# Attention and multiplicative feed-forward on one core: the k·v product of the next batch moved into the two-level gates, in front of a q·kv product

## The chip, the cores and the metric

One core of a Trainium2 chip runs the whole program in one launch. The metric is the device time of that core in microseconds (us), median of the runs shown. All matrix products are float32. The engines are named as in the profile: PE (TensorE; PEld its weight loads), DVE (VectorE), ACT (ScalarE), POOL (GpSimd), SP (SyncE, which here issues most DMAs).

## The reference, cut to what matters

```python
batch, n_heads, seq, head_dim = (8, 8, 576, 64)
kv  = np.einsum('bhsd,bhse->bhde', k, v)          # 64x64 per head and batch
out = np.einsum('bhsd,bhde->bhse', q, kv)
rms = np.sqrt(np.mean(out * out, axis=-1, keepdims=True) + 1e-06)
x   = (out / rms * g_norm)                        # -> (8*576 tokens, 512)
a = x @ w1                                        # 512 -> 1024
b = x @ w2
h = a * b @ w3                                    # 1024 -> 1024
return h @ w_out                                  # 1024 -> 512
```

No step is non-linear between `w3` and `w_out`, so the kernel multiplies these two once, at the start, and then has two products per token: the gates (x times w1 and w2, multiplied elementwise) and the projection (times w3·w_out).

## The kernel before, in words

**Groups.** The 4608 tokens are worked on in nine groups of 512. Groups T = 0 to 6 and T = 7 hold the first 512 tokens of one batch each; T = 8 holds the 64 tokens left over of all eight batches. The order (`groups`, L1135) is 0, 1, ..., 6, 8, 7. While group T goes through its gates, the attention of batch b = T + 1 is computed in pieces in between, by `steps(b)` (L573).

**Fewer products by Strassen-Winograd.** The gates and the projection are written as seven products of half-size blocks instead of eight (`winograd`, L698). For T in `IN_TWO` (2 to 6, 8 and 7) the gates of the first three quarters of the features use two such levels, 49 products for 64 (`gates_of_two`, L948, matmuls of 128x128 by 128 columns at L976), with a one-level `gates` call for feature part p = 2 ahead of them and one for p = 3 behind them (128x128 by 256 columns, L708). Then `project_twice` (L1189) does the projection in two levels (L1223).

**Pieces.** Each of the three gate stages calls `between()`, which runs the next piece of `steps(b)`: pieces 0 and 1 in the gates of p = 2; pieces 2 to 5 in the two-level gates (after the third and the sixth of seven products, for each of w1 and w2); pieces 6 and 7 in the gates of p = 3. For b > 2 (`in_two`) they hold: piece 1, `begin_kv(1)` and `finish(0)` of batch b; piece 3, for odd b, `product_left` (L423, matmul L432); piece 4, `finish(1)`; piece 6, `begin_kv(0)` of batch b + 1.

**What these do.** `begin_kv(g)` (L480) calls `kv(g)` (L326): 36 matmuls of 64x64 (L335) into two PSUM banks, then six small ACT copies into `kv_sb` (L343, L345), and issues the loads of the next k and v (L104, on SP). `finish(h)` calls `product(h)` (L399): 32 matmuls of 64x64 (L413) into two banks, and `norm` (L374): per bank an ACT square (L380) and a DVE reduction (L381), then an ACT square root (L385), a DVE reciprocal (L387) and two DVE multiplications (L390). For b > 2 both squares go to one buffer, `sq0`, so that the second waits for the first reduction.

**PSUM.** Eight banks in two pools: `ps_mm` with five and `ps_at` with three. The two-level gates hold all five of `ps_mm`; of these `mm[0]` is used last by the second product of the second half (`plan`, L951), and read by `add_seven` (L1029, L1030). `product(1)` takes both its banks from `ps_at` for b > 2, and the `winograd` call of p = 3 takes its first bank, r1, from `ps_mm`.

**What sets the order.** PE, POOL and SP run in the order of the code. DVE runs in the order of the code from the gates of p = 3 to the end of the projection, and in an order that a planner makes elsewhere; ACT always in an order that the planner makes. In `gates` a DVE addition (L859) and multiplication (L860) make each block of the result; ACT copies (L726) keep the intermediate sums. Behind them, on DVE, come the sums that the projection reads: for its first product `sum_inner(0)`, for its second and third `sum_inner(1, 2)` (L1181, L1182, L1183 and L1185; the second call is the one of 128x512), and the sums over the first three feature parts (L1069 to L1072).

Of the kernel before, what the change touches and what calls it, by code (L numbers as in the profile page):

```python
# [22 lines left out]
def kernel(  # L23
# [36 lines left out]
    B, H, S, D = q.shape  # L60
# [4 lines left out]
    FIRST_OF_TWO = 2  # L65
# [18 lines left out]
    def bank(pool, tag):  # L84
        return pool.tile([P, 512], FP32, name=tag, tag=tag)
# [28 lines left out]
    NF = KF // 2  # L114
# [203 lines left out]
    def attention(b):  # L318
# [80 lines left out]
        def product(h):  # L399

            of_mm = b and not (h and b > FIRST_OF_TWO)
            o_ps = [bank(*((ps_mm, "mm") if of_mm else (ps_at, "at"))), bank(ps_at, "at")]
            for m in range(4):
                r, e = 2 * h + m // 2, m % 2
                for i in range(2):
                    n = 2 * m + i
                    for t in range(2):
                        tokens = slice(t * L, (t + 1) * L)  # L410
                        for l in range(2):
                            rows = slice(l * D, (l + 1) * D)
                            nc.tensor.matmul(  # L413
                                o_ps[l][tokens, n * D:(n + 1) * D],
                                lhsT=qT[r][rows, e, i, tokens],
                                rhs=kv_b[rows, m // 2 ^ l, e, h, :],
                                start=True,
                                stop=True,
                            )
            xn = st[h] = work.tile([P, 2, 2, 4, D], FP32, name="xn", bufs=1)  # L420
            return norm(o_ps, [xn[:, :, l].rearrange("p i m d -> p m i d") for l in range(2)])
# [90 lines left out]
    def batch(b):  # L512
        if b not in batches:
            batches[b] = attention(b)
        return batches[b]
# [57 lines left out]
    def steps(b):  # L573

        a = batch(b)
        a.start()
        more = b + 1 < B  # L580
        fs, ends = ([[] for _ in range(8)] for _ in range(2))

        def turn(i, f, *args, next_group=False):

            t = []

            def begin():
                t.append(f(*args))
                next(t[0])
                next(t[0])  # L590

            fs[i].append((begin,))
            (to_end if next_group else ends[i + 1]).append((lambda: all_of(t[0]),))

        if to_end:

            ends[0] += [(lambda: nc.gpsimd.tensor_copy(tick, late["p5"][:, 0, 0:1]),), *to_end]
        to_end.clear()
        odd = b % 2
        by_scalar, in_two = b >= FIRST_OF_TWO, b > FIRST_OF_TWO  # L600
        if b == 1:
            early.extend(a.q_two_by_dma(r) for r in (0, 1))
            q_first = list(early)
            fs[0].append((a.begin_kv, 0))

            def end_first():
                for t in q_first:
                    with tc.issue_after(copies["u3"][-1].ins):
                        next(t)
                    all_of(t)  # L610

            ends[1].append((end_first,))
        fs[2 if b == 1 else 1] += [(a.begin_kv, 1), (a.finish, 0)]
        if b == 1:
            last = {}

            def begin(name, behind, f, *args):
                last[name] = f(*args)
                with tc.issue_after(copies[behind][-1].ins):
                    next(last[name])  # L620
                next(last[name])

            def end(name, behind):
                with tc.issue_after(copies[behind][-1].ins):
                    next(last[name], None)
                all_of(last[name])

            fs[2] += [(begin, f"q{r}", "u2", a.q_two_by_dma, r) for r in (2, 3)]
            fs[3].append((begin, "left", "u3", a.q_left_by_dma))
            fs[4].append((begin, "x", "u3", a.x_by_dma, 0, nc.scalar.copy))  # L630
            ends[4] += [(end, "q2", "p1"), (end, "q3", "p5")]
            ends[5] += [(end, "x", "u2"), (end, "left", "u3")]
        elif by_scalar:
            turns_by_scalar(b)
        else:
            turn(1, a.q_two_by_dma, 2, 3)
            turn(2, a.x_by_dma, 0)
            if odd:
                turn(1, a.q_left_by_dma)
        second = 5 if b == 1 else 4  # L640
        if more:
            fs[6 if in_two else second].append((batch(b + 1).begin_kv, 0))
        fs[second].append((a.finish, 1))
        if odd:
            fs[3 if in_two else second + 1].append((a.product_left,))
        if b == 1:
            turn(6, a.x_by_dma, 1)
            turn(7, a.x_left_by_dma, next_group=True)
        else:
            if not by_scalar:  # L650
                turn(5, a.x_by_dma, 1)
            if odd:
                turn(5, a.x_left_by_dma, next_group=more)
        if more and not by_scalar:
            turn(7 if b == 1 else 5, batch(b + 1).q_two_by_dma, 0, 1, next_group=True)
        if more:
            fs[7 if odd else 0].append((load_q_left, b + 1))
        return iter([lambda s=e + f: [f(*args) for f, *args in s] for e, f in zip(ends, fs)])
# [38 lines left out]

    def winograd(  # L698
        lhsT, rhs, chunks, done, between=lambda: None, keep_u3=True, after=lambda: None,
        places=(2, 1),  # L700
    ):


        def product(a_name, b_name, to=None):
            ps = to if to is not None else bank(ps_mm, "mm").rearrange("p (u n) -> p u n", u=2)
            for u in range(2):
                for c in range(chunks):
                    nc.tensor.matmul(  # L708
                        ps[:, u, :],
                        lhsT=lhsT(a_name, u, c),  # L710
                        rhs=rhs(b_name, c),

                        start=(u == 0 and c == 0 and to is None),
                        stop=(c == chunks - 1),
                        skip_group_check=True,
                    )
            after()
            return ps

        def keep(name, ps):  # L720
            if name == "p1":
                t = pair_of_sums[:, 0].rearrange("p s c t -> p (s c) t")
            else:
                t = late_slots(places[name != "p5"])
            t = t[:, 0:4, :].rearrange("p (u a) n -> p u (a n)", u=2)
            copies.setdefault(name, []).append(nc.scalar.copy(t, ps))  # L726
            run_slot((stage[0], name), copies[name][-1])
            late[name] = t
            return t

        r1 = product("a11", "b11")
        p1 = keep("p1", r1)
        r2 = product("s1", "t1")
        p5 = keep("p5", r2)
        product("s2", "t2", r1)
        u2 = keep("u2", r1)
        between()
        product("s4", "b22", r2)
        done("c12", r2, u2)
        product("s3", "t3", r1)  # L740
        done("c22", p5, keep("u3", r1) if keep_u3 else r1)
        r3 = product("a12", "b21")
        done("c11", r3, p1)
        between()
        product("a22", "t4", r1)
        done("c21", r1, None)
# [97 lines left out]
    def gates(T, p, between, ready=lambda name: None):  # L844
        def done(name, one, two):
            multiply(name, one, two)
            ready(name)

        def multiply(name, one, two):

            dst = ab[int(name[1]) - 1][:, p, int(name[2]) - 1, :]
            if two is None:
                c = late_pool.tile([P, N], FP32, name="c21")
                copied = nc.scalar.copy(c, one[:, 0, :])  # L854
                run_slot((stage[0], name), copied)
                adds.setdefault(name, []).append(nc.vector.tensor_mul(dst, c, one[:, 1, :]))
                return
            c = late_pool.tile([P, 2, N], FP32, name="c")
            adds.setdefault(name, []).append(nc.vector.tensor_add(c, one, two))  # L859
            nc.vector.tensor_mul(dst, c[:, 0, :], c[:, 1, :])  # L860

        winograd(
            lambda name, w, c: wa[p][name][:, w, c, :],
            lambda name, c: xb[T][name][:, c, :],
            NP // 2, done, between, T == 0 or p + 1 < NF,
            places=(2, 1) if T not in IN_TWO else (0, 1) if p + 1 == NF else (2, 0),
        )


# [721 lines left out]
```

## Time and profile before

| | |
|---|---|
| median of 3 runs (lowest, highest) | 747.46 us (747.32, 747.8) |
| the profiled execution: its own time | 747.49 us |
| its span, first to last instruction | 745.7 us |
| granted TensorE clock | 1.000 |
| POOL busy | 21.8 us, 3% of the span |
| largest group by line: L708 matmuls from `xT`, `w_sb` | x480, 110.2 us |

The profiled execution's time is 1.8 us longer than its span; that part lies outside of the first and last instruction. Each float32 matmul of the code shows as two matmul records in the trace. A record's duration contains the pipeline behind it, so that records overlap: how long work takes on PE is read from start to start. In a row of the timeline, "x16" means that 16 records of one kind follow each other, the first number is the start in us from the span's start, the second how long the row lasts.

| group | T = 2 | T = 3 | T = 4 | T = 5 | T = 6 |
|---|---|---|---|---|---|
| batch of the pieces, b | 3 | 4 | 5 | 6 | 7 |
| `product(1)` in the two-level gates, start | 270.60 | 343.57 | 417.37 | 490.35 | 564.15 |
| k·v of b + 1 in the gates of p = 3, start | 283.32 | 356.30 | 430.10 | 503.07 | none |

### The profile page before, as it was taken

What the parts mean: (1) busy time and instruction counts of PE and PEld (TensorE: products, weight loads), DVE (VectorE), ACT (ScalarE), POOL (GpSimd) and SP (SyncE); (2) the same over time, 40 slices, a digit from 0 to 9 for tenths busy, and PEclk for the clock granted to TensorE, in tenths of its full rate; (3) what the DMA queues carried; (4) which work ended last, traced back from release to release, by engine and by line L of the source; (5) the groups of instructions that cost most, each with busy time, mean ns of one, the idle gap of its engine ahead of it and who ended that gap; (6) DMA issues with size and microseconds to landing.
All of it is one profiled execution on the core that took longest, in us unless ns stands there. A gap on an engine that the chain in (4) does not pass through costs nothing.

```text
span 745.7 us, 16754 instructions
## 1 busy us (share of the span) xinstructions
PE 737.6 (99%) x6843; PEld 658.4 (88%) x6843; DVE 633.1 (85%) x1212; ACT 371.3 (50%) x638; POOL 21.8 (3%) x29
## 2 busy tenths in 40 slices
PE   8999999999999999999999999999999999999998
PEld 6455788888899999999999999999999999999997
DVE  7987998957868699979996999799969987997797
ACT  6787868424552575256526752575267313212321
POOL 0000000132000000010000000000001000000000
PEclk9999999999999999999999999999999999999999
DMA  9996944499999689867986898579847662465454
GB/s 319 364 313 207 258 104 124 124 325 298 283 307 327 167 219 269 310 167 234 279 280 168 253 295 270 175 244 279 277 106 218 207 225 87 157 229 165 134 199 135
DMA packets 135456, 169.65 MB, mean 228 GB/s; under 512 B 78036, under 2 KB 110804, under 8 KB 135380
## 3 DMA queue, kind: packets, MB, share of 16 engines
q1 hardware_dynamic: 132928, 154.16, 68.9%
q10 hardware_dynamic: 2452, 14.42, 5.7%
q8 instruction: 54, 0.88, 0.5%
q14 instruction: 22, 0.18, 0.1%
HBM read 130.55 MB, written 20.71 MB: 203 GB/s over the span
## 4 chain that ended last, share of the span: by engine, by line
PE 92%; DVE 3%; DMA 3%; ACT 1%; issue 0%; SPq 0%; POOL 0%; ACTq 0%; DVEq 0%
PE mm L708 36%; PE mm L1223 22%; PE mm L976 21%; PE mm L682 7%; PE at L335 2%; PE at L413 1%; DMA raw<-in_moe_w_out_dram 1%; DMA w3o_sb<-w3o_l 1%; PE at L669 1%; PE mm L413 1%; DVE c L859 1%; DMA raw<-in_moe_w_dram 0%; DVE w_sb L172 0%; DMA out_dram<-raw 0%; PE at L1266 0%
## 5 line engine op out<-in xcount | busy, mean ns | idle before, releaser
L1025 ACT COPY slots<-mm 128x512 f32<-128x512 f32 x88 | 51.6, 586 | 131.8 <-PE mm L1223 73.7
L708 PE MATMUL mm<-xT,w_sb 128*128 128x256 f32 x480 | 110.2, 379 | 0.0
L708 PEld LDWEIGHTS mm<-xT,w_sb 128*128 128x128 f32 x480 | 90.4, 190 | 12.1 <-issue 0.5
L708 PE MATMUL mm<-xc,ws 128*128 128x256 f32 x352 | 79.8, 380 | 0.0
L708 PEld LDWEIGHTS mm<-xc,ws 128*128 128x128 f32 x352 | 66.9, 190 | 9.4 <-ACT inner_sums L726 0.4
L726 ACT COPY slots<-mm 128x512 f32<-128x512 f32 x61 | 35.7, 586 | 76.7 <-PE mm L708 54.6
L682 PE MATMUL mm<-chunks,ab 128*128 128x512 f32 x128 | 60.8, 606 | 0.6 <-DVE chunks L172 0.6
L1029 DVE TENSOR_TENSOR slots<-mm,slots 128x512 f32<-128x512 f32 x66 | 45.3, 686 | 17.7 <-PE mm L976 17.3
L1026 ACT COPY slots<-mm 128x384 f32<-128x384 f32 x88 | 42.4, 482 | 24.9 <-PE mm L1223 22.3
L976 PE MATMUL mm<-ws,w3o_sb 128*128 128x128 f32 x350 | 54.0, 275 | 0.0
L1223 PE MATMUL mm<-w3o_sb,ab 128*128 128x128 f32 x368 | 48.7, 275 | 0.5 <-DMA w3o_sb<-w3o_l 0.5
L381 DVE TENSOR_REDUCE inv<-sq 128x8 f32<-128x512 f32 (+1 forms) x40 | 24.6, 629 | 26.4 <-ACT sq L380 26.2
L976 PEld LDWEIGHTS mm<-ws,w3o_sb 128*128 128x128 f32 x350 | 46.4, 192 | 0.0
L1223 PEld LDWEIGHTS mm<-w3o_sb,ab 128*128 128x128 f32 x368 | 45.4, 192 | 1.1 <-issue 0.7
L1223 PE MATMUL mm<-w3o_sb,raw 128*128 128x128 f32 x340 | 43.5, 275 | 0.0
L708 PE MATMUL mm<-xc,w_sb 128*128 128x256 f32 x176 | 42.5, 385 | 0.9 <-ACT slots L726 0.9
L682 PEld LDWEIGHTS mm<-chunks,ab 128*128 128x128 f32 x128 | 21.6, 190 | 22.3 <-issue 14.3
L1223 PEld LDWEIGHTS mm<-w3o_sb,raw 128*128 128x128 f32 x340 | 40.7, 192 | 0.0
L708 PE MATMUL mm<-xT,ws 128*128 128x256 f32 x160 | 38.5, 384 | 0.0
L708 PEld LDWEIGHTS mm<-xc,w_sb 128*128 128x128 f32 x176 | 32.7, 190 | 6.3 <-ACT slots L726 1.7
L1030 DVE TENSOR_TENSOR slots<-mm,slots 128x384 f32<-128x384 f32 x66 | 36.4, 552 | 0.9 <-PE mm L1223 0.9
L854 ACT COPY c<-mm 128x256 f32<-128x256 f32 x22 | 8.2, 371 | 53.7 <-PE mm L708 53.7
(230 smaller groups left out, 1634.8 us busy)
## 6 DMA issues: line engine op xcount, KB each, us to landing
w3o_sb<-w_l SPq DMA_DIRECT2D x21, 896.0 KB, 5.5
w3o_sb<-w3o_l SPq DMA_DIRECT2D x18, 896.0 KB, 4.6
raw<-in_moe_w_dram SPq DMA_DIRECT2D x31, 512.0 KB, 7.5
raw<-w3o_l SPq DMA_DIRECT2D x15, 896.0 KB, 4.9
w3o_sb<-w3o_l ACTq DMA_DIRECT2D x14, 896.0 KB, 5.1
k_sb<-in_k_dram SPq DMA_DIRECT2D x16, 576.0 KB, 4.6
v_sb<-in_v_dram SPq DMA_DIRECT2D x16, 576.0 KB, 6.2
q_sb<-in_q_dram SPq DMA_DIRECT2D x32, 256.0 KB, 4.4
```

Source lines behind the costliest of these rows:

```text
L335: nc.tensor.matmul(ps[r * D:(r + 1) * D, :], lhsT=k_sb[rows, r, cols], rhs=v_sb[rows, r, cols], start=(j == 0), stop=(j == JS - 1),)
L381: adds["norm"] = nc.vector.tensor_reduce(out=inv[:, i], in_=sq.rearrange("p (h d) -> p h d", d=D), axis=AX.X, op=ALU.add)
L413: nc.tensor.matmul(o_ps[l][tokens, n * D:(n + 1) * D], lhsT=qT[r][rows, e, i, tokens], rhs=kv_b[rows, m // 2 ^ l, e, h, :], start=True, st ...
L682: nc.tensor.matmul(sums_ps[half][m], lhsT=w3T[half, c][:, m, :], rhs=chunks[:, c, 1, :], start=(c == 0), stop=(c == KF - 1),)
L708: nc.tensor.matmul(ps[:, u, :], lhsT=lhsT(a_name, u, c), rhs=rhs(b_name, c),  start=(u == 0 and c == 0 and to is None), stop=(c == chunks ...
L726: copies.setdefault(name, []).append(nc.scalar.copy(t, ps))
L976: nc.tensor.matmul(ps[place // 4][:, place % 4, :], lhsT=x, rhs=y, start=new and place // 4 not in seen, stop=True, skip_group_check=True,)
L1025: nc.scalar.copy(z[:, 0:4], ps[0])
L1026: return nc.scalar.copy(z[:, 4:7], ps[1][:, 0:3])
L1029: nc.vector.tensor_add(z[:, 0:4], ps[0], z[:, 0:4])
L1030: nc.vector.tensor_add(z[:, 4:7], ps[1][:, 0:3], z[:, 4:7])
L1223: nc.tensor.matmul(ps[place // 4][:, place % 4, :], lhsT=x[:, c, :], rhs=y[:, c, :], start=new and place // 4 not in seen, stop=(c == 1), ...
```

## The change

For b = 3 to 6, that is in groups T = 2 to 5, `begin_kv(0)` of batch b + 1 moves from piece 6 to piece 4, directly in front of `finish(1)`. So the k·v matmuls, which stood alone in the gates of p = 3, now stand directly ahead of the q·kv matmuls in the two-level gates. This needs two banks of `ps_at` at that place, and so the banks are dealt differently: `product(1)` of these batches takes its first bank from `ps_mm` (it gets `mm[0]`), and the first bank of the `winograd` call of p = 3 comes from `ps_at`. By the same condition batch 0, at the start of the program, takes the first bank of its two products from `ps_mm`.

```diff
-            of_mm = b and not (h and b > FIRST_OF_TWO)
+            of_mm = b < B - 1 or h == 0
             o_ps = [bank(*((ps_mm, "mm") if of_mm else (ps_at, "at"))), bank(ps_at, "at")]
...
         if more:
-            fs[6 if in_two else second].append((batch(b + 1).begin_kv, 0))
+            fs[second].append((batch(b + 1).begin_kv, 0))
         fs[second].append((a.finish, 1))
...
-        places=(2, 1),
+        places=(2, 1), first=None,
...
         def product(a_name, b_name, to=None):
-            ps = to if to is not None else bank(ps_mm, "mm").rearrange("p (u n) -> p u n", u=2)
+            new = to is None or to is first
+            ps = bank(ps_mm, "mm").rearrange("p (u n) -> p u n", u=2) if to is None else to
...
-                        start=(u == 0 and c == 0 and to is None),
+                        start=(u == 0 and c == 0 and new),
...
-        r1 = product("a11", "b11")
+        r1 = product("a11", "b11", to=first)
         p1 = keep("p1", r1)
+        first = None
...
             places=(2, 1) if T not in IN_TWO else (0, 1) if p + 1 == NF else (2, 0),
+            first=(
+                bank(ps_at, "at").rearrange("p (u n) -> p u n", u=2)
+                if T in IN_TWO and p + 1 == NF and T + 2 < B else None
+            ),
```

In the built programs, per changed group: on PE the 36 matmuls of L335 stand ahead of the 32 of L413, and the gates of p = 3 are without them. On ACT the six copies of L343 and L345 stand ahead of the first square (L380) of `finish(1)`. On SP the two loads of L104 stand ahead of the transposition of the left-over tokens (odd b) and of the first three loads for the projection (L1152), instead of behind the four transpositions of the gates of p = 3. The order on DVE and on POOL is the same.

## The prediction, made before the changed kernel was run

> **What bounds the kernel now.** I read the page first: its busy line, then the chain that ended last, then the timelines of PE, DVE and ACT around every 64x64 product.
>
> ```profile
> PE 737.6 (99%) x6843; PEld 658.4 (88%) x6843; DVE 633.1 (85%) x1212; ACT 371.3 (50%) x638; POOL 21.8 (3%) x29
> PE 92%; DVE 3%; DMA 3%; ACT 1%; issue 0%; SPq 0%; POOL 0%; ACTq 0%; DVEq 0%
> ```
>
> PE sets the end: it is busy 99% of the span and 92% of the chain lies on it. A us that PE no longer spends is gained, as long as no other engine makes it wait in its place. DVE, at 85%, is the one to watch. In the timeline of PE from group T = 2 on, starts follow each other at fixed steps: 16 records of 128x256 take 3.46 us (241.35 to 244.81), 0.216 each; 12 of 128x128 take 1.34, 0.112 each. The steps are broken in two kinds of place only: around 64x64 products, and once in group T = 6.
>
> **What the change takes from PE.** The first view is the timeline of PE around the k·v product alone, in the last gates of T = 2:
>
> ```profile
> 279.77 3.62 PE L708 MATMUL mm<-xc,ws 128*128 128x256 f32 x16
> 283.32 1.28 PE L335 MATMUL at<-v_sb,k_sb 64*64 64x64 f32 x72
> 284.53 1.99 PE L708 MATMUL mm<-xT,ws 128*128 128x256 f32 x8
> 286.36 3.62 PE L708 MATMUL mm<-xT,w_sb 128*128 128x256 f32 x16
> ```
>
> From 279.77 to 286.36 are 6.59 us, in which 24 large records should take 24 x 0.216 = 5.18. The interruption costs 1.41 us. Next, q·kv alone, in the two-level gates of the same group:
>
> ```profile
> 270.28 0.39 PE L976 MATMUL mm<-ws,w3o_sb 128*128 128x128 f32 x2
> 270.60 1.16 PE L413 MATMUL at<-kv_sb,qT 64*64 64x64 f32 x64
> 271.69 0.71 PE L976 MATMUL mm<-xc,w3o_sb 128*128 128x128 f32 x4
> 272.24 0.83 PE L976 MATMUL mm<-ws,w3o_sb 128*128 128x128 f32 x6
> ```
>
> From 270.28 to 272.24 are 1.96 us for six records, 0.67: the interruption costs 1.29. Last, both in one, as `begin_kv(1)` and `finish(0)` already stand in the first gates:
>
> ```profile
> 246.53 3.62 PE L708 MATMUL mm<-xT,w_sb 128*128 128x256 f32 x16
> 250.08 1.28 PE L335 MATMUL at<-v_sb,k_sb 64*64 64x64 f32 x72
> 252.22 1.99 PE L708 MATMUL mm<-xc,w_sb 128*128 128x256 f32 x8
> 254.05 0.39 PE L976 MATMUL mm<-xT,w_sb 128*128 128x128 f32 x2
> ```
>
> From 246.53 to 254.05 are 7.52 for 24 large records (5.18): 2.34. Joining the two saves 1.41 + 1.29 - 2.34 = **0.36 us per group**, 1.44 in the four groups T = 2 to 5. What goes is one entry into the small products and one return from them. The figure for the joint case comes from between 256-column matmuls; between 128-column ones entry and return cost the same to 0.01 (the L335 in T = 3 to 5 repeat 1.41, the L413 1.29).
>
> **What the moved step does elsewhere.** Times below count from the start of the interruption in the two-level gates (270.60 in T = 2).
>
> *PE after it* runs 2.34 - 1.29 = 1.05 late until the gates of p = 3, where 1.41 falls away.
>
> *ACT and DVE*: the six kv copies now stand ahead of the first square, and with them the whole norm. The joint case shows the price; the timeline of the first gates of T = 2, all engines:
>
> ```profile
> 251.41 0.21 ACT L343 COPY kv_sb<-at 128x64 f32<-128x64 f32 x1 [2.36 <-PE at L335]
> ...
> 252.74 0.60 ACT L380 ACTIVATE sq<-mm 128x512 f32<-128x512 f32 x1
> ...
> 254.78 0.69 DVE L381 TENSOR_REDUCE inv<-sq 128x8 f32<-128x512 f32 x1 [0.72 <-ACT sq L380]
> ```
>
> The copies begin 1.33 after the k·v product (250.08) and take 1.33, the square follows at 2.66; the second reduction, which waits for the second square, which waits for the first reduction (one `sq0`), begins at 4.70. All five joint cases from T = 2 on give these numbers to 0.03. With q·kv alone that second reduction begins at 3.41 to 3.46. So DVE's work behind it starts **1.24 later**, against 1.05 for PE.
>
> *Where that matters.* From the second reduction on DVE has an unbroken list: two additions of the two-level gates, reciprocal, the norm's multiplications, the finishing sums, the block results of p = 3, `sum_inner(0)`, then `sum_inner(1, 2)`, whose blocks are weights of the projection's second product. In T = 2 to 5 DVE stands idle in the gates of p = 3 (0.26, 0.51 and 0.12 us ahead of the three L859 of T = 2, the first two put down to PE's L708): PE's k·v product gives it time to catch up. The change takes that time away. Group T = 6 shows what then happens, for its gates of p = 3 have no k·v. DVE, then PE, there:
>
> ```profile
> 567.61 0.69 DVE L381 TENSOR_REDUCE inv<-sq 128x8 f32<-128x512 f32 x1 [0.66 <-ACT sq L380]
> ...
> 588.98 0.69 DVE L1185 TENSOR_TENSOR raw<-raw 128x512 f32<-128x512 f32 x1
> ...
> 586.81 1.50 PE L1223 MATMUL mm<-raw 128*128 128x128 f32 x12
> 588.15 1.68 PE L1223 MATMUL mm<-raw,inner_sums 128*128 128x128 f32 x12
> 589.72 0.71 PE L1223 MATMUL mm<-raw 128*128 128x128 f32 x4
> 590.27 0.39 PE L1223 MATMUL mm<-w3o_sb,raw 128*128 128x128 f32 x2
> ```
>
> DVE needs 21.37 us from one to the other, with no gap that PE causes. The 12 records at 588.15 take 1.57 instead of 1.34, and the four at 589.72, whose weights L1185 has just ended (589.67), 0.55 instead of 0.45: PE loses **0.33**. It is the only wait of PE on DVE from T = 2 on; T = 2 has the same records at 296.00 to 297.79 without loss.
>
> After the change T = 2 to 5 look like T = 6, with DVE another 1.24 - 1.05 = 0.19 behind PE: the loss is 0.33 + 0.19 = **0.52 per group**. The same directly: L1185 would begin at 4.70 + 21.37 = 26.07, end at 26.76, and PE's four records start 0.05 behind it at 26.81; undisturbed they would start at 297.34 - 270.60 + 1.05 - 1.41 = 26.38. That is 0.43, and 0.10 more because the next weights couldn't be loaded ahead.
>
> Sum per group: -0.36 + 0.52 = +0.16; four groups +0.64. On the profiled execution, 747.49 (its span of 745.7 and 1.8 around it; the median of the three runs is 747.46), that makes **748.1 us**.
>
> **The edits that I cost at nothing.** *Bank `mm[0]` for q·kv*: its last reader, the L1030 at 269.93, ends at 270.48, before k·v even begins; were it late, PE would wait for the difference. *The `ps_at` bank as r1 in p = 3*: read out by the kv copies at 2.64, wanted at 8.5. The two further banks of `ps_at` for odd b were left by the L390 of the left-over tokens at 269.42, 1.2 ahead. *Batch 0*: the L682 matmuls of that stage have 0.6 us of idle time in all, put down to DVE and not to a bank, so freed banks bring nothing; the bank that is taken is one of five of which four are held. *SP*: k and v are issued at about 1.36 (251.44 in the joint case), in front of the first L1152 (274.89 in T = 2, 4.29 in); they land in 4.4 to 6.2 us, and the projection first reads an L1152 at 291.54, so there is room for a collision of 10 us. What was behind them in p = 3, the q left over and an L1152 at 292.04, comes no later. *ACT in p = 3* loses six copies from a stretch in which it next stands idle for 4.31.
>
> [...] Here the copying (1.33 on ACT for 1.10 on PE) isn't itself what PE waits for; it delays a third engine.
>
> **Rivals.**
> 1. *The loss is that of T = 6 only*, 0.33: when DVE's extra 0.19 is swallowed by some wait that I took for work. Then -0.03 per group, 747.4. For it: T = 6 is measured, the 0.19 is put together. Against it: no gap in T = 6's list to swallow it.
> 2. *The change does what it says and no more*: no new wait, -1.44, 746.05. It needs DVE to keep its slack; against it stands T = 6. If only half of the loss came, 747.1.
> 3. *Slower*: ACT isn't free when the k·v product ends. In T = 1 and in the first groups the kv copies begin 1.72 (195.72) to 3.42 (134.66) behind their product instead of 1.33, and the square with them; each 0.1 there is 0.1 more for PE in each group. At the 1.72 of T = 1 it would be 0.39 x 4 = 1.56 more, 749.7; at 3.42, 8.4 more, 756.5. In the two-level gates ACT's last copy before (L1026) ends at 0.64, which leaves 0.69 spare. It decides, against the bound below, from copies that begin 0.21 late.
>
> The unknown is PE's new wait: its ends are nothing (746.05) and the 749.7 of rival 3's nearest row (756.5, the farthest, needs ACT to be held for 2 us by work that isn't there). I take 0.52 because the row that it is nearest to, T = 6, has the same DVE list, instruction by instruction.
>
> **How the numbers follow.** Forecast 0.58; rival 1 0.18; rival 2 with the half-way cases 0.10; rival 3 0.14. A measurement of this kernel tells about 0.2%, 1.49 us, from no change: under 745.97 is faster, over 748.95 slower. Forecast, rival 1 and most of rival 2 lie within; the rest of rival 2 (a saving somewhat larger than 1.44) is 0.03; rival 3 beyond 748.95 is 0.13. So faster 0.03, same 0.84, slower 0.13. The range, 747.0 to 749.4, leaves out the lower part of rival 2 and the upper half of rival 3, together under 0.2.
>
> **What would show it.** On PE: no L335 in p = 3 of T = 2 to 5, the joint interruption 2.34 long, and a loss of about 0.5 at the projection's records `raw,inner_sums`, put down to DVE. On DVE: the second L381 4.7 after the start, no idle time ahead of the three L859 of p = 3. On ACT: the first L343 at 1.33. The forecast is wrong if DVE still shows idle time there (then rival 2), if the L343 comes late (rival 3), or if a new wait on a DMA or a bank appears at L335 or L413.

## The result, and the profile after

| | before | after |
|---|---|---|
| median of 21 runs each (lowest, highest) | 747.93 us (747.06, 748.98) | 749.03 us (748.27, 751.75) |
| the profiled execution, and its span | 747.49, 745.7 us | 748.81, 747.0 us |

The ratio is 1.0018 (95% interval 1.0012 to 1.0024): by it the changed kernel is about 1.35 us slower (0.9 to 1.8); the medians differ by 1.10. The forecast was 748.1, 0.64 above before. Direction and range held; the size was about half of what was measured.

In the code after the change lines shift a little: L708, L859, L976, L1029, L1185 and L1223 of before are L709, L861, L982, L1035, L1191 and L1229. The page of the changed kernel, its busy line and its chain of work that ended last, by engine:

```profile
PE 738.1 (99%) x6843; PEld 658.6 (88%) x6843; DVE 632.1 (85%) x1212; ACT 372.4 (50%) x638; POOL 21.8 (3%) x29
PE 94%; DVE 3%; DMA 2%; ACT 1%; issue 1%; SPq 0%; ACTq 0%; DVEq 0%
```

PE still sets the end. "issue", time for which the profile shows no reason, reads 1% after 0%; that is rounding (3.87 us of the chain against 3.72 before), but one piece of 0.47 us is new and matters below. Now the places that the prediction named. The timeline of PE around the joint interruption of T = 2, then that of ACT and of DVE at the same place:

```profile
270.51 0.39 PE L982 MATMUL mm<-ws,w3o_sb 128*128 128x128 f32 x2
270.83 1.28 PE L335 MATMUL at<-v_sb,k_sb 64*64 64x64 f32 x72
...
272.97 0.71 PE L982 MATMUL mm<-xc,w3o_sb 128*128 128x128 f32 x4
273.52 0.72 PE L982 MATMUL mm<-ws,w3o_sb 128*128 128x128 f32 x5
```

```profile
272.16 0.21 ACT L343 COPY kv_sb<-at 128x64 f32<-128x64 f32 x1 [0.68 <-PE at L335]
...
273.50 0.60 ACT L380 ACTIVATE sq<-mm 128x512 f32<-128x512 f32 x1
```

```profile
275.48 0.69 DVE L381 TENSOR_REDUCE inv<-sq 128x8 f32<-128x512 f32 x1 [0.66 <-ACT sq L380]
...
278.16 0.69 DVE L390 TENSOR_TENSOR xn<-mm,inv 128x512 f32<-128x512 f32 x1 [0.18 <-ACT xT L308]
...
296.85 0.68 DVE L1191 TENSOR_TENSOR raw<-raw 128x512 f32<-128x512 f32 x1
```

From 270.51 to 273.52 are 3.01 us, in which six records of 128x128 should take 0.67: the interruption costs 2.34, as forecast, and the L335 of p = 3 is gone. The kv copies begin 1.33 after the start (272.16), the second reduction 4.65, and L1191 26.02, where the prediction had 1.33, 4.70 and 26.07. There is no DVE idle time of note left in front of the three L861 of p = 3 (0.10 us at most, ahead of the one at 288.96). What PE pays shows in the last product of p = 3 of T = 2, by its weight loads, and then at the projection:

```profile
289.70 1.59 PEld L709 LDWEIGHTS at<-xc,w_sb 128*128 128x128 f32 x8 [0.25 <-DVE c L861]
...
294.66 1.50 PE L1229 MATMUL mm<-raw 128*128 128x128 f32 x12
296.00 1.69 PE L1229 MATMUL mm<-raw,inner_sums 128*128 128x128 f32 x12
297.58 0.71 PE L1229 MATMUL mm<-raw 128*128 128x128 f32 x4
298.13 1.06 PE L1229 MATMUL mm<-w3o_sb,raw 128*128 128x128 f32 x8
```

Twelve records at 296.00 take 1.58 instead of 1.34, the four at 297.58 0.55 instead of 0.45: 0.34. Another 0.12 is lost ahead of it, where the last product of p = 3 waits for DVE's L861 (from 289.47 to 290.02 two records take 0.55 instead of 0.43). Together 0.46.

What no step of the prediction had is in T = 4. The timeline of PE there, the end of the joint interruption:

```profile
417.85 1.28 PE L335 MATMUL at<-v_sb,k_sb 64*64 64x64 f32 x72
...
419.83 0.22 PE L413 MATMUL at<-kv_sb,qT 64*64 64x64 f32 x1
420.51 0.21 PE L413 MATMUL mm<-kv_sb,qT 64*64 64x64 f32 x1 [0.47 <-issue]
420.51 0.33 PE L413 MATMUL at<-kv_sb,qT 64*64 64x64 f32 x2
420.77 0.71 PE L982 MATMUL mm<-xc,w3o_sb 128*128 128x128 f32 x4
```

Three records before the end of the burst PE stops, for nothing that the profile shows: no bank, no data, no DMA of the kernel. Other records of the burst mostly follow each other at 0.01 to 0.04, at 0.15 at most; here 0.68 pass. The interruption costs 3.12 instead of 2.34.

The sum, from the start of one group's joint interruption in p = 2 to the next group's (250.08, 323.88, 396.86, 470.65 and 543.63 in the kernel before), as difference to the kernel before in us:

| | up to T = 2 | T = 2 | T = 3 | T = 4 | T = 5 | sum of T = 2 to 5 |
|---|---|---|---|---|---|---|
| after | +0.23 | +0.11 | +0.13 | +0.71 | +0.12 | +1.07 |

What lies ahead of T = 2 differs from one profiled execution to the next, whatever the kernel (PE's wait at the first projection of T = 1, mostly for a DMA, was 0.54 in this profile of before, 0.82 here, and 0.2 to 1.7 in the runs below), so these columns, and not whole times, carry the reading of the experiments.

### The profile page after: what moved, and what is told of

Same layout as the page of the kernel before. It is cut to its first block, busy times and chain, and to the rows that moved or that the text cites. A ratio compares the mean times of both kernels' runs of the same rounds, so it can differ in the third digit from the quotient of the medians.

```text
span 747.0 us, 16752 instructions
## 1 busy us (share of the span) xinstructions
PE 738.1 (99%) x6843; PEld 658.6 (88%) x6843; DVE 632.1 (85%) x1212; ACT 372.4 (50%) x638; POOL 21.8 (3%) x29
## 4 chain that ended last, share of the span: by engine, by line
PE 94%; DVE 3%; DMA 2%; ACT 1%; issue 1%; SPq 0%; ACTq 0%; DVEq 0%
PE mm L709 33%; PE mm L1229 22%; PE mm L982 21%; PE mm L682 7%; PE at L709 4%; PE at L335 2%; PE mm L413 2%; DMA w3o_sb<-w3o_l 1%; PE at L669 1%; DMA raw<-in_moe_w_out_dram 1%; DVE ab L162 1%; PE at L413 1%; DVE w_sb L172 0%; PE at L1272 0%; DVE c L861 0%
## 5 line engine op out<-in xcount | busy, mean ns | idle before, releaser
L1031 ACT COPY slots<-mm 128x512 f32<-128x512 f32 x88 | 51.7, 587 | 130.4 <-PE mm L1229 48.3
L709 PE MATMUL mm<-xT,w_sb 128*128 128x256 f32 x416 | 95.7, 379 | 0.0
L709 PEld LDWEIGHTS mm<-xT,w_sb 128*128 128x128 f32 x416 | 78.4, 190 | 10.8 <-issue 0.5
L709 PE MATMUL mm<-xc,ws 128*128 128x256 f32 x320 | 72.7, 379 | 0.0
L727 ACT COPY slots<-mm 128x512 f32<-128x512 f32 x57 | 33.5, 588 | 76.8 <-PE mm L709 54.6
L709 PEld LDWEIGHTS mm<-xc,ws 128*128 128x128 f32 x320 | 60.7, 190 | 8.4 <-ACT inner_sums L727 0.2
L1035 DVE TENSOR_TENSOR slots<-mm,slots 128x512 f32<-128x512 f32 x66 | 45.3, 686 | 17.5 <-PE mm L982 17.3
L982 PE MATMUL mm<-ws,w3o_sb 128*128 128x128 f32 x350 | 53.9, 275 | 0.0
L381 DVE TENSOR_REDUCE inv<-sq 128x8 f32<-128x512 f32 (+1 forms) x40 | 24.6, 628 | 31.5 <-ACT sq L380 31.5
L1229 PE MATMUL mm<-w3o_sb,ab 128*128 128x128 f32 x368 | 48.7, 275 | 0.8 <-DMA w3o_sb<-w3o_l 0.8
L1229 PEld LDWEIGHTS mm<-w3o_sb,ab 128*128 128x128 f32 x368 | 45.4, 192 | 1.4 <-DVE raw L1064 1.0
L982 PEld LDWEIGHTS mm<-ws,w3o_sb 128*128 128x128 f32 x350 | 46.4, 192 | 0.0
L1229 PE MATMUL mm<-w3o_sb,raw 128*128 128x128 f32 x340 | 43.5, 275 | 0.0
L1229 PEld LDWEIGHTS mm<-w3o_sb,raw 128*128 128x128 f32 x340 | 40.7, 192 | 0.0
L709 PE MATMUL mm<-xT,ws 128*128 128x256 f32 x160 | 38.1, 381 | 0.0
L709 PE MATMUL mm<-xc,w_sb 128*128 128x256 f32 x144 | 35.0, 386 | 0.9 <-ACT slots L727 0.9
L709 PEld LDWEIGHTS mm<-xT,ws 128*128 128x128 f32 x160 | 30.0, 190 | 4.4
L308 ACT COPY xT<-xn 128x1024 uint16<-128x1024 uint16 x28 | 32.5, 1167 | 2.0 <-DMA xn<-xT 2.0
```

Of the source, the lines that this page charges most:

```text
L308: copy(words(dst), src)
L381: adds["norm"] = nc.vector.tensor_reduce(out=inv[:, i], in_=sq.rearrange("p (h d) -> p h d", d=D), axis=AX.X, op=ALU.add)
L709: nc.tensor.matmul(ps[:, u, :], lhsT=lhsT(a_name, u, c), rhs=rhs(b_name, c),  start=(u == 0 and c == 0 and new), stop=(c == chunks - 1), s ...
L982: nc.tensor.matmul(ps[place // 4][:, place % 4, :], lhsT=x, rhs=y, start=new and place // 4 not in seen, stop=True, skip_group_check=True,)
L1031: nc.scalar.copy(z[:, 0:4], ps[0])
L1035: nc.vector.tensor_add(z[:, 0:4], ps[0], z[:, 0:4])
```

## The experiments

Every edit below is against the kernel after, with "..." where lines are left out; a comment in it may name the run. Each ratio is to the kernel before as measured again beside that run (medians of 748.04 to 748.37), so that a run's median can't be set against the 747.93 above.

**Two theories.** A: the 0.46 per group is DVE's lateness, as predicted, in two parts: 0.33 because PE no longer gives DVE a break in p = 3, and the rest because the kv copies push the norm back. B: the 0.78 in T = 4 is PE waiting for its own instructions. For B the page has a line in its third part, on a queue that it calls "instruction":

```profile
q8 instruction: 54, 0.88, 0.5%
```

54 packets in 0.88 MB are 16.3 KB each. PE's records in the trace, weight loads and control instructions counted in, are 13835, or 256 for each packet: an estimate, for no view says that all 54 are PE's. An instruction block, below, is 256 of PE's records in a row. And the joint burst, 72 + 64 matmul records with as many weight loads, is 272 instructions in 2.1 us, where the matmuls around it need 15 us (128x128, 0.112 a record) or 29 us (128x256, 0.216) for as many. Rival to B: the stop belongs to the data of T = 4.

**1 and 2. Shift the instruction index.** Five, or one, of the nine warm-up matmuls at the start are left out; four instructions each.

```diff
-        keep_warm(9)
+        keep_warm(4)     # x1_five_fewer; keep_warm(8) in x2_one_fewer
```

> The kernel after, with five of the nine warm-up matmuls at its very start left out (they multiply the identity by itself and their results are read by nobody), so that every later TensorE instruction has an index 20 lower; nothing else is touched. Theory B: the 0.47 us of idle TensorE ahead of the L413 at 420.51 in T = 4 is TensorE waiting for its own next block of instructions, because the block's end fell 5 instructions before the end of the burst of 272 small instructions. Shifted by 20, the end falls into the large matmuls behind the burst: the gap put down to issue is gone, the joint interruption of the two-level gates of T = 4 is 2.34 as in T = 2, 3 and 5 instead of 3.12, and the time is about 0.7 us below that of the kernel after, some 0.5 us above the kernel before. Rival: the gap belongs to the data of T = 4 (a bank, the load of k and v), and then it stays at the same L413 with 3.12, and the time stays that of the kernel after, about 1.35 above the kernel before.

> The kernel after, with one of the nine warm-up matmuls at its start left out (identity by itself, read by nobody): every later TensorE instruction has an index 4 lower. A control for the shift by 20. Theory B: the block's end now falls one instruction before the end of the burst in T = 4, or on it, and most of the gap stays (0.3 to 0.5 us of idle time at the last L413 or at the large matmul behind it); time within 0.3 us of the kernel after. Rival (the start of the kernel sets the phase in some other way, so that any change there removes the gap): no gap here either.

x1_five_fewer: 749.26 us, ratio 1.0015 (1.0006 to 1.0024). In T = 4 the interruption is 2.34, the stop is gone, and that group is 0.10 slower than before. But now T = 5 has one. The timeline of PE there:

```profile
493.50 0.22 PE L413 MATMUL at<-kv_sb,qT 64*64 64x64 f32 x1
494.04 0.27 PE L413 MATMUL mm<-kv_sb,qT 64*64 64x64 f32 x1 [0.32 <-issue]
```

x2_one_fewer: 749.32, ratio 1.0014 (1.0005 to 1.0023); stops in T = 4 (0.56 more than 2.34) and in T = 5 (0.92). Counted through the records, the stops of all three kernels stand at index 8129, 9666, 8129 and 9666: 193 and 194 modulo 256, at the same index whichever product is there. The data of T = 4 are out. The expectation was right on the shift's effect and wrong on the total: a shift removes one stop and can make another.

**3. The k·v product behind the q·kv product.**

```diff
+            if not in_two:
+                fs[second].append((batch(b + 1).begin_kv, 0))
         fs[second].append((a.finish, 1))
+        if more and in_two:
+            fs[second].append((batch(b + 1).begin_kv, 0))
```

> The kernel after, with the k v product directly behind the second q kv product of the two-level gates in place of directly in front of it. Still one joint interruption, but the six kv copies on ScalarE now come behind the squares of the norm. Theory A (the loss at the projection's second product comes from the norm, held up by the copies): the second L381 begins at 3.4 to 3.5 us after the start of the interruption instead of 4.70, VectorE has the 1.2 us back, and the 0.46 to 0.49 per group at the projection's records with inner_sums goes down to at most 0.33 (that of T = 6, where k v is not in p = 3 either), since TensorE has still lost the time in p = 3 that it used to give VectorE. The interruption stays 2.34. So -0.36 + (0.1 to 0.33) per group, 0.1 to 1.0 us faster than the kernel before, without a wait for instructions. Rival: the loss comes from the k v product having left p = 3 alone and the order of the copies is of no matter; then the losses stay 0.46 to 0.49 and the time is that of the kernel after. A second rival: the copies of L1025 or the kv copies come late on ScalarE in the new order, and TensorE waits in the two-level gates themselves for a bank; then the time is above that of the kernel after.

756.57 us, ratio 1.0111 (1.0097 to 1.0125); T = 2 to 5 are 1.9 to 2.4 slower each. The second rival held. The planner puts the kv copies, and the root of the norm, ahead of the copies of the p5 sums on ACT (p5 is the fourth of the seven products), and PE waits for these. And the burst of T = 4 has its stop again. The timeline of PE, T = 2 and T = 4 (L985 and L1034 here are L982 and L1031):

```profile
277.87 0.71 PE L985 MATMUL mm<-xT,raw 128*128 128x128 f32 x4 [0.77 <-ACT slots L1034]
...
423.98 0.62 PE L335 MATMUL at<-v_sb,k_sb 64*64 64x64 f32 x26
426.40 0.33 PE L335 MATMUL at<-v_sb,k_sb 64*64 64x64 f32 x4 [1.80 <-issue]
```

Index 8129 once more, now in an L335, since the products have changed places: the stop goes with the place in the stream, not with the operation.

**4. The banks alone.** The k·v product stays in p = 3, the other edits are in.

```diff
-            fs[second].append((batch(b + 1).begin_kv, 0))
+            fs[6 if in_two else second].append((batch(b + 1).begin_kv, 0))
```

> The changes of banks alone: q kv takes its first bank from mm in all batches but the last, and the gates of p = 3 of the groups concerned take r1 from ps_at, as in the kernel after; the k v product stays alone in p = 3, as in the kernel before. The prediction's value for these edits: nothing, so the time of the kernel before within 0.2 us, with the interruptions at 1.41 and 1.29. Rival: taking a bank from another pool makes TensorE wait somewhere; then there is a gap put down to ScalarE or VectorE at L413, L335 or the first product of p = 3, and part of the 1.35 us of the kernel after shows here.

748.38 us, ratio 1.0005 (0.9996 to 1.0014); T = 2 to 5 agree with the kernel before to 0.00 each. The bank edits are free.

**5 and 6. A shift chosen to clear all four bursts, and one chosen to hit T = 3.** 16 or 24 products of 32x32 are added to the warm-up.

```diff
...
-        keep_warm(9)
+        keep_warm(9, 16)     # y1_shift64: 16 products more; 24 in y4_shift96
```

> The kernel after, with 16 products of 32x32 added to the warm-up at the start (their results are read by nobody), so that every later TensorE instruction has an index 64 higher. Theory B after the first runs: TensorE stops at a fixed place of its instruction stream, at an index of 193 or 194 modulo 256, when a whole block of 256 instructions is used up in about 2 us, and that happens only where a joint burst of 272 begins within some 20 instructions of such a place. Counted from the burst's first instruction, the place lay at 136, 105, 11 and 236 in T = 2 to 5 of the kernel after; with 64 more it lies at 72, 41, 203 and 172, clear of both ends. So no stall put down to issue anywhere, the joint interruption 2.34 in all four groups, each group 0.10 to 0.13 slower than in the kernel before, and in sum about 0.45 us above the kernel before in place of 1.1 to 1.35 (the start of the kernel and the wait for a DMA in T = 1 differ from run to run by some tenths). Rival: a stall comes up at another place.

> The same with 24 products of 32x32 in place of 16: indices 96 higher. The place modulo 256 then lies at 40, 9, 171 and 140 of the joint bursts of T = 2 to 5. Theory B says: the stall moves to T = 3, at the L413 some 265 instructions into its burst (around 346 us), 0.3 to 0.7 us or more long, and T = 2, 4 and 5 have none. Rival: the stall belongs to T = 4 and 5, and T = 3 has none, as in every run so far.

y1_shift64: no stop, 2.34 in all four groups, +0.13, +0.12, +0.12, +0.11. In whole times this is not to be seen: 749.22 us, ratio 1.0015 (1.0006 to 1.0023), so that what the stop costs is read from the columns alone. In the profiled execution the burst that begins at 174.33 in the kernel after begins 0.26 later, and T = 1 waited 1.55 for DMAs. y4_shift96 (one run, 750.38 us): the stop is in T = 3, whose burst had none in any other kernel. The timeline of PE (L418 is L413):

```profile
347.52 0.22 PE L418 MATMUL at<-kv_sb,qT 64*64 64x64 f32 x1
348.17 0.21 PE L418 MATMUL mm<-kv_sb,qT 64*64 64x64 f32 x1 [0.43 <-issue]
```

Index 6593, again 193 modulo 256; 0.75 more than 2.34. T = 4 and 5 have none. A smaller stop that was not expected stands behind the burst of T = 2, at index 5058: it lengthens the two-level gates by 0.37, of which DVE, given that time, returns more than half, and the group is 0.24 slower than before (by the sum, the loss behind it is 0.24 + 0.36 - 0.37 = 0.23 and not 0.46). B is shown in this: where the stop was put, it came. That PE waits there for its own instructions is the author's reading of the place and of queue q8; no view states it. Which places give a small stop was not forecast. Each kernel was profiled once, so how often a stop comes in other executions is not shown; that three kernels stop at index 8129 and two at 9666 speaks for its being regular.

**7. The loss split in two.** The banks as in x4_banks, and the k·v product of p = 3 left out.

```diff
         def begin_kv(g, left_out=False):
-            kv(g)
+            if not left_out:     # left out in p = 3 of T = 2 to 5
+                kv(g)
...
-            fs[second].append((batch(b + 1).begin_kv, 0))
+            fs[6 if in_two else second].append((batch(b + 1).begin_kv, 0, in_two))
```

> The changes of banks alone, with the k v product of the second half of the batches 4 to 7 left out altogether (72 records and six copies in p = 3 of T = 2 to 5; the loads stay, and the later products read an older kv): the computation is not the reference's. It splits the loss in two. By the prediction 0.33 of it comes only from TensorE no longer giving VectorE a break in p = 3, and the rest, 0.13 to 0.19, from the norm that begins 1.24 late against 1.05 of TensorE. Here the break is gone and the norm is not late: TensorE saves 1.41 in p = 3 plus the product's own 0 (it is inside the 1.41), and loses 0.33 at the projection's records with inner_sums in each of T = 2 to 5, as T = 6 does. So each group 1.08 faster than in the kernel before, 4.3 in sum. Rival: no loss at the projection, 1.41 per group, 5.6 in sum; then the whole loss came from the late norm.

One run, 744.84 us. T = 2, 3 and 5 are 1.08, 1.11 and 1.12 faster than before (T = 4 has a wait of 1.27 for a DMA at 446.09 of its own). The timeline of PE at the projection of T = 2:

```profile
294.81 1.67 PE L1230 MATMUL mm<-raw,inner_sums 128*128 128x128 f32 x12
296.38 0.71 PE L1230 MATMUL mm<-raw 128*128 128x128 f32 x4
296.93 1.28 PE L1230 MATMUL mm<-w3o_sb,raw 128*128 128x128 f32 x10
```

From 294.81 to 296.93 are 2.12 us for 16 records that should take 16 x 0.112 = 1.79: 0.33 is lost with the norm as early as before (0.29 to 0.34 in the other groups). This part comes from the missing break alone; the remaining 0.13 of the 0.46, found by difference, goes with the late norm.

**8. k·v behind, its copies last.** x3_behind with the six copies issued behind the last copies of the two-level gates, and the shift of y1_shift64.

```diff
...
+            fs[second].append((batch(b + 1).begin_kv, 0, True))      # products now, copies later
+            slots.setdefault((1, 6), []).append((batch(b + 1).end_kv,))
```

> The k v product behind the second q kv product, as in x3_behind, with its six copies on ScalarE put behind the copies of the last two-level product (L1031, L1032 of w = 1, n = 6), where ScalarE stood idle for 1.25 us in the kernel before; and the shift by 64 instructions of y1_shift64. Theory A: the norm begins as early as in the kernel before (second L381 at 3.4 to 3.5 us of the interruption) while TensorE is 1.05 us later, so VectorE is about 0.85 us further ahead than in T = 6 of the kernel before, and the loss at the projection's records with inner_sums is gone. Each group is then 0.35 us faster than in the kernel before, 1.4 in sum: a ratio near 0.998. Rival: the copies of the p5 sums come late on ScalarE in this order too and TensorE waits for them as in x3_behind (0.5 to 0.8 twice in a group); or the loss at the projection stays at 0.3 to 0.5, because it does not hang on the norm.

751.54 us, ratio 1.0044 (1.0032 to 1.0057); +0.91, +0.67, +0.94, +0.67. The reductions came as early as expected, and the loss at the projection stayed at 0.35, with PE waiting at the start of p = 3 (0.47 in T = 2) and in it (0.44) as well. The timeline of DVE in T = 2 (L392, L398, L401, L313 are L381, L387, L390, L308) says why:

```profile
274.12 0.69 DVE L392 TENSOR_REDUCE inv<-sq 128x8 f32<-128x512 f32 x1 [0.72 <-ACT sq L391]
275.19 0.25 DVE L398 RECIPROCAL inv<-inv 128x16 f32<-128x16 f32 x1 [0.38 <-ACT inv L396]
...
278.16 0.69 DVE L401 TENSOR_TENSOR xn<-mm,inv 128x512 f32<-128x512 f32 x1 [1.34 <-ACT xT L313]
```

The second reduction is at 3.50 of the interruption (270.62), 1.15 earlier than after the change, but the first multiplication at 7.54, later than its 7.33. It writes the one buffer `xn`, which two ACT copies of the other half (L313) still read, and those stand behind the root and the p5 copies. So the first form of A, in which the second reduction sets the list, falls. Its mended form, on which the next runs were built: the first multiplication sets it, and that needs the norm **and** those two copies.

**9 to 11. The ACT order mended, in two steps.** z1_norm_later issues the root and what follows it behind the p5 copies; z4_free_shift splits the shift over two waits at the start; z3_xt_earlier also takes one of the two L308 ahead of the squares.

```diff
-        fs[second].append((a.finish, 1))
+            t = []
+            fs[second].append((lambda: (t.append(a.product(1)), next(t[0])),))
+            slots.setdefault((1, 3), []).insert(0, (lambda: all_of(t[0]),))
...
-        keep_warm(9, 16)     # z4_free_shift: keep_warm(9, 8), and keep_warm(2, 8) further on
...
-            x_begins, x_ends = ((0, 3), (0, 3)), ((1, 3), (1, 3))
+            x_begins, x_ends = ((0, 3), (0, 3)), ((1, 2), (1, 3))     # z3_xt_earlier
```

> y3_behind_later with the rest of the norm (the root L385 and what follows it) issued behind the copies of the p5 sums of the same gates in place of in front of them; the k v product behind the q kv product, the kv copies behind the last two-level copies, and 64 more TensorE instructions at the start, as there. In y3_behind_later VectorE stood idle for 1.34 us ahead of the norm's first multiplication, until ScalarE had copied the last xT out of the buffer xn that the multiplication overwrites; those copies stood behind the root and the p5 copies. Theory A in its mended form (what sets VectorE's list is this multiplication, which needs the norm and the buffer): here it begins 6.6 to 7.0 us after the start of the interruption, where it began at 6.13 in the kernel before, 7.33 in the kernel after and 7.54 in y3_behind_later, with TensorE 1.05 later than in the kernel before. The loss at the projection's records with inner_sums falls from 0.46 to between 0 and 0.2, the wait for the bank at the first product of p = 3 (0.06 to 0.34 in y3_behind_later) is gone, and each group is 0.15 to 0.35 faster than in the kernel before: ratio near 0.9985. Rival: TensorE waits for something else in p = 3 (0.13 at the second weights of it in y3_behind_later), and the gain stays away; the time is then that of the kernel before or above.

> z1_norm_later with its 16 products of 32x32 split in two lots of 8, one ahead of each of the two waits of TensorE on VectorE in the kernel's first 20 us (0.9 us each in the kernel before), so that the shift of the instruction index is hidden there in place of costing about 0.3 us. The groups T = 2 to 5 as in z1_norm_later, 0.04 to 0.13 faster each than in the kernel before, 0.43 in sum, no stall put down to issue. So about 0.4 us faster than the kernel before, a ratio near 0.9995 that the interval of these rounds will hardly separate from 1. Rival: the indices in the split form let a boundary fall into a burst again; then 0.4 to 0.8 of stall shows in one group.

> z4_free_shift with one of the two copies of xT that read the buffer xn (L308) issued behind the copies of the second product instead of behind those of p5, ahead of the squares. Mended theory: the norm's first multiplication waits for these copies; with one of them out of the way it begins near 6.0 to 6.4 us after the start of the interruption in place of 7.07, the 0.15 left of the loss at the projection and the 0.075 at p = 3 go, and the group gains the full 0.35: 1.4 in sum, a ratio near 0.998. Rival: the copy delays the squares by 0.6 us and with them the p5 copies behind, and TensorE waits for these in the two-level gates (0.2 to 0.6 per group); then it is slower than z4_free_shift.

| | T = 2 | T = 3 | T = 4 | T = 5 | sum | median, ratio to before |
|---|---|---|---|---|---|---|
| z1_norm_later | -0.13 | -0.04 | -0.13 | -0.13 | -0.43 | 747.96, 0.9996 (0.9987 to 1.0005) |
| z4_free_shift | -0.13 | +0.10 | -0.12 | -0.12 | -0.27 | 748.19, 0.9998 (0.9990 to 1.0007) |
| z3_xt_earlier | -0.36 | -0.34 | -0.36 | -0.36 | -1.42 | 746.92, 0.9988 (0.9979 to 0.9997) |

z1_norm_later fell short of the 0.15 to 0.35 expected per group. z3_xt_earlier is faster than the kernel before, by about 0.9 us in whole times (0.2 to 1.6) and 1.42 in the columns. The timeline of its DVE and that of its PE in T = 2 (L1252 and L1214 are L1229 and L1191; the interruption begins at 271.23):

```profile
277.28 0.68 DVE L401 TENSOR_TENSOR xn<-mm,inv 128x512 f32<-128x512 f32 x1
...
296.69 0.68 DVE L1214 TENSOR_TENSOR raw<-raw 128x512 f32<-128x512 f32 x1
```

```profile
294.94 1.50 PE L1252 MATMUL mm<-raw 128*128 128x128 f32 x12
296.28 1.50 PE L1252 MATMUL mm<-raw,inner_sums 128*128 128x128 f32 x12
297.62 0.61 PE L1252 MATMUL mm<-raw 128*128 128x128 f32 x4
298.07 0.72 PE L1252 MATMUL mm<-w3o_sb,raw 128*128 128x128 f32 x5
```

The first multiplication begins at 6.05, and the steps of the projection are 1.34 and 0.45: nothing is lost, and the 0.36 of the joint interruption is kept whole in each group. Set side by side, T = 2 where nothing else is said, with the last sum of `sum_inner(1, 2)` (L1191 after, L1185 before) beside the multiplication, both in us after the start of the interruption:

| | first L390 | L1185 or L1191 | lost in the group |
|---|---|---|---|
| z3_xt_earlier | 6.05 | 25.46 | 0.00 |
| z1_norm_later | 7.07 | 25.77 | 0.22 |
| z3_xt_earlier, T = 6, with 1.05 added, since PE is so much earlier there | 6.57 | 25.87 | 0.32 |
| before, T = 6, with 1.05 added | 7.20 | 25.88 | 0.33 |
| after | 7.33 | 26.02 | 0.46 |
| y3_behind_later | 7.54 | 26.82 | 1.26 |

The last column follows the second number and not the first: wherever PE loses, the loss is the start of that last sum less 25.56, to 0.01. So the mended form of A holds for y3_behind_later and not as a rule. What counts is when the list ends: every wait of DVE up to there adds to it, wherever it stands. In z1_norm_later the multiplication no longer waits for the copies of xT; DVE stands idle ahead of it for the root and for a product of PE. In T = 6 of z3_xt_earlier DVE takes the multiplication one addition earlier, 0.63 sooner than in the kernel before, and the list ends as late as there. The timeline of DVE, T = 2 of z1_norm_later and T = 6 of z3_xt_earlier:

```profile
276.53 0.25 DVE L398 RECIPROCAL inv<-inv 128x16 f32<-128x16 f32 x1 [0.53 <-ACT inv L396]
...
278.27 0.69 DVE L1058 TENSOR_TENSOR slots<-mm,slots 128x512 f32<-128x512 f32 x1 [0.34 <-PE mm L1005]
```

```profile
568.90 1.29 DVE L401 TENSOR_TENSOR xn<-at,inv 128x512 f32<-128x512 f32 x2
...
588.20 0.68 DVE L1214 TENSOR_TENSOR raw<-raw 128x512 f32<-128x512 f32 x1
```

What z4_free_shift lost in T = 3 is a small stop of the kind of B, at index 6593 behind the burst (0.22 from 348.54 on): the rival of its expectation, with a smaller size.

## Why the prediction was right in direction, and wrong in size

- *The saving of a joint interruption*, 0.36 per group: measured 0.35, and all of it was to be had (z3_xt_earlier).
- *The loss*, 0.52 per group: measured 0.46 in T = 2, 0.48 in T = 3 and 0.47 in T = 5. The instants on ACT and DVE were right to 0.05. The 0.33 taken from T = 6 came back as 0.33 in y5_no_kv, so splitting the loss into a missing break and a late norm was right. The second term is 0.13 and not 0.19, since the second reduction came at 4.65 and not at 4.70. And 0.12 of the loss is paid earlier, in p = 3.
- *Which event sets DVE's list*: the prediction followed the second reduction. After the change both roads end together (the multiplication waits only 0.18 for the copy of xT), so the number came out right, and that was luck: y3_behind_later and z1_norm_later show other waits further down the list that the prediction did not look for.
- *The edits costed at nothing* (banks): 0.00 in x4_banks. The loads of k and v did no harm in T = 2 to 5.
- *The step that failed* is the sentence "between 128-column ones entry and return cost the same to 0.01". It carried the joint 2.34 over from the gates of p = 2. Entry and return do cost the same. But the joint burst has 272 instructions, more than the 256 from one place at 193 or 194 modulo 256 to the next, and in T = 4 0.68 pass between two records at such a place. So the interruption costs 2.34 in three groups and 3.12 in T = 4. By the table that is 0.60 more than the other groups (the stop gives DVE time, so T = 4 loses 0.29 and not 0.46 behind it: the records of L1229 from 443.68 on take 1.52 and 0.55 for 1.34 and 0.45). Four groups at 0.11 to 0.13 would be about +0.48; with the 0.60 they make 1.07.
- *The rivals*: the time came near rival 3's 749.7, but its mechanism is not there (the copies begin at 1.33, not late). A new wait at L335 or L413 was named as a sign against the forecast, for a DMA or a bank; the wait that came is neither.
- *The whole time* lay in the range, but not by the forecast's sum alone: of the 0.93 between 748.1 and 749.03, 0.47 is the kernel before, whose median of 21 runs is 747.93 and not 747.46, the stop, for which the sum had no term, is 0.60, and the rest of the sum came out 0.16 smaller (0.48 for 0.64).

## What to carry to other kernels

Joining two bursts of small products saves one entry and one return (0.35 us here), but price what each engine behind it gets later: here the ACT order decided whether the same PE saving was lost, kept in part or kept whole. Where a burst runs through more than 256 instructions in about 2 us (here 272 in 2.1), count along PE's instructions: a stop put down to "issue" at the same index modulo 256 (here 193 and 194) is the sign, and a shift of the stream moves it, as five products fewer and 24 more did here. When an early reduction doesn't help, look at every wait behind it down to the end of the list, above all at an instruction that overwrites a buffer, and ask who still reads it.

## What the runs showed of the hardware that was not expected

Queue q8 instruction moved 54 packets during the run, in the kernel before from 33.20 us on, in the kernel after from 37.37. Counting packets and instruction blocks in order, the first packet put down to the block that begins at index 449 (193 modulo 256), in the kernel before no block was entered sooner than 4.66 us after the start of its packet. In the kernel after it was 2.34 at the stop in T = 4 (packet at 418.17, PE goes on at 420.51), where PE had entered the block ahead at 417.92, and 4.12 or more at every other block. The stops inside a burst, six in x1_five_fewer, x2_one_fewer, x3_behind, y4_shift96 and the kernel after, lengthened an interruption by 0.54 (x1_five_fewer, T = 5) to 2.12 us (x3_behind, T = 4). From the second packet on, in both kernels, the packet for a block started between 3.9 us before and 5.4 us after PE entered the block ahead of it. What sets the start of a packet within these bounds stays open: in the gates of p = 2 of T = 2 the kernel before runs through a block in 1.87 us without a stop (250.09 to 251.96), the packet for the next block having started at 246.71, 3.4 us ahead of 250.09, and none of the runs shows why that one started early and the one at 418.17 did not.
